# Attention and two gated layers on one core: more key tiles turned from fp32r copies, fewer rows of exponentials, query sums copied twice

## The chip, the core and the metric

One core of one Trainium2 chip runs the whole program. The metric is the device time of one execution in microseconds (us), the median of the runs shown. Engines: TensorE (PE; its weight loads are PEld), VectorE (DVE), ScalarE (ACT), GpSimd (POOL) and SyncE (SP), whose queue issues nearly all DMAs.

## What is computed

The reference, cut to what matters:

```
q, k, v: (2, 8, 1152, 64)
q_pool = q.reshape(B, H, S // 2, 2, D).mean(axis=3)
scores = (1 / sqrt(D)) * q_pool @ k.T
attn   = softmax(scores, axis=-1)
x      = (attn @ v), heads side by side      # (1152, 512)
x      = g1(x @ w_in1) @ w_out1              # 512 -> 2048 -> 512
out    = g2(x @ w_in2) @ w_out2              # the same shape, g2 = SiLU
```

There are 16 heads. Each has 576 pooled queries (four tiles of 128, and 64 that are put together with the 64 of the neighbouring head) and 1152 keys (nine tiles of 128).

## The kernel before

Every product is made in two or three fp32r matmuls of a high and a low part, so each operand is split into both parts first. The program has two halves that overlap a little: attention, to about 277 us of the span, and the two layers, which fill TensorE to the end.

Attention, per head. `inputs(h)` loads k, q and v; splits k (ACT and POOL), turns it on TensorE in three groups of three transposes and evacuates them into `kk`; adds the two query rows of a pool on POOL into one half of `qs` (line 481), copies that half into the other by a DMA (line 488), turns `qs` by four fp32 transposes (line 496) and scales and splits the outcome into `qm`. For head 0 the sum is made twice over by one DVE instruction instead of the DMA (line 483). `scores(h, t)` multiplies a query tile t with the 1152 keys in three banks (line 570), DVE evacuates them into a row tile `p` with a running minimum (line 577), and ACT takes exponentials in place (line 590). There are 8 such `p` tiles of [128, 1152] fp32, 4608 bytes a partition each, four for a head. Line 597 copies key tiles 4 and 5, and 6 to 8, of each finished `p` by DMA into `pr0` and `pr1`, which are typed fp32r: there is one buffer of each for all heads. `values(h)` goes over the nine key tiles: four transposes (one per query tile), from `p` in fp32 with `ident` (line 630) for tiles 0 to 3, from `pr` in fp32r with `ident_r` (line 634) for tiles 4 to 8; the bank is split into `thl` (ACT with DVE, or ACT with POOL), and two matmuls of 512 columns add it to the head's sum (line 647). `tails` does the same for the two joined 64-query rests, with line 676 and line 685.

Order. All instructions are first listed as operations with a due time, a cost (occupancy and latency per engine) and the buffers that they need. `plan_out` (line 265) simulates the engines with these costs and always takes what can start first, by due time among equals; the program is then written out in that order, and each engine, SP too, takes its instructions in order and waits where one is not ready. A copy of n key tiles is charged 0.2 + 0.18 n us on SP and 2.7 + 0.2 n us until it has landed; four turns from a copy are charged 0.27 us on TensorE, four from `p` 0.436 us.

The lines that the change touches:

Of the kernel before, what the change touches and what calls it, by code (L numbers as in the profile page):

```python
# [8 lines left out]
F32 = mybir.dt.float32  # L9
F32R = mybir.dt.float32r  # L10
# [8 lines left out]
def fused_kernel(  # L19
# [11 lines left out]
    nc = tc.nc  # L31
    B, H, S, D = q.shape
# [3 lines left out]
    P = 128  # L36
    KC = S // P
    NM = SQ // P
# [12 lines left out]
    THL = 4  # L51
    PF = 2
    SLACK = 0.2
    WARM = 7
    COPIED = ((4, 2), (6, 3))
    AHEAD = 3.0
    KINDS = ("psum", "pool", "psum", "pool", "psum", "pool", "psum", "pool", "pool")
    KEVAC = [[("ACT", 0.37, 0.484), ("DVE", 0.476, 0.547)]] * 3
# [8 lines left out]
    ident = const.tile([P, P], F32, name="ident")  # L67
    make_identity(nc, ident)
    ident_r = const.tile([P, P], F32R, name="ident_r")
# [72 lines left out]
    banks = [psum.tile([P, 512], F32, name=f"bank{i}") for i in range(8)]  # L142
# [103 lines left out]
    room = {}  # L246

    def op(target, ways, deps=(), bufs=(), both=False):

        if isinstance(ways, tuple):  # L250
            ways = [ways]
        o = Op(target, ways, [d for d in deps if d is not None], list(bufs), both)
        for b in o.bufs:
            b.left += 1
        ops.append(o)
        return o
# [87 lines left out]
    with ExitStack() as at, ExitStack() as keys, ExitStack() as prep:  # L344
        fixed = at.enter_context(tc.tile_pool(name="fixed", bufs=1))
        pp = at.enter_context(tc.tile_pool(name="pp", bufs=1))
# [3 lines left out]
        nat = prep.enter_context(tc.tile_pool(name="nat", bufs=1))  # L350

        def several(pool, n, shape, dt, name):
            return [pool.tile(shape, dt, name=f"{name}{i}") for i in range(n)]
# [4 lines left out]
        kraws = several(nat, 2, [P, KC, D], F32, "kraw")  # L358
        vraws = several(nat, 1, [P, KC, D], F32, "vraw")
        khls = several(nat, 2, [P, KC, 2, D], F32R, "khl")  # L360
        qss = several(nat, 2, [P, NM, 2, D], F32, "qs")
        kks = several(qk, 3, [P, KC, P], F32R, "kk")
        qms = [several(qk, 2, [P, NM * P], F32R, f"qm{i}") for i in range(2)]
        qts = [several(qk, 2, [P, 3, QT], F32R, f"qt{i}") for i in range(2)]
        ps_ = several(pp, 2 * NM, [P, S], F32, "p")
        pts = several(pp, 1, [P, S], F32, "pt")

        prs = [pp.tile([P, NM, n * P], F32R, name=f"pr{i}") for i, (_, n) in enumerate(COPIED)]
# [3 lines left out]
        y2s = several(pp, 2, [P, NM * P], F32, "y2")  # L372
        rbs = several(pp, 2, [P, NM * P], F32, "rb")
        ztail = fixed.tile([P, P], F32, name="ztail")
        tiny = fixed.tile([P, 1], F32, name="tiny")
        room.update(qraw=2, kraw=2, vraw=1, khl=2, qs=2, kk=3, qm=2, qt=2, qtraw=2, qts=1, p=2 * NM, pt=1, **{f"pr{i}": 1 for i in range(len(COPIED))}, thl=THL, pf=PF, vhl=2)
        room.update(y2=2, rb=2, z=1, b=6, y=2, w=1)

        def clear(what):
# [9 lines left out]
        khl, kk, qs, qm, qt, vhl, kraw, qraw, vraw, qtraw, o_lqt = ({} for _ in range(11))  # L389
        o_k, o_q, o_qt, o_v, o_p, o_y, o_inv, o_z = ({} for _ in range(8))  # L390
        p_of, y2_of, rb_of, pr_of, o_r = {}, {}, {}, {}, {}
# [17 lines left out]
        def inputs(h):  # L409

            b, hd = divmod(h, H)
# [15 lines left out]
            pr, odd = divmod(h, 2)  # L427
# [29 lines left out]
            for g in range(3):  # L457
                bank = Buf("b")
# [13 lines left out]
                ways = [(e, occ, lat, (lambda e=e, ev=evac: ev(e)())) for e, occ, lat in KEVAC[g]]  # L472
                o_k[h].append(op(t2 + 0.5, ways, [o], [bank, kb2]))

            qb, bank, mb = Buf("qs"), Buf("b"), Buf("qm")
            qm[h] = mb

            def split_q(e):
                t = qraws[qr.slot]
                if h:  # L480
                    e.tensor_add(qss[qb.slot][:, :, 0], t[:, :, 0], t[:, :, 1])
                else:
                    e.tensor_add(qss[qb.slot], *(t[:, :, r].unsqueeze(2).to_broadcast([P, NM, 2, D]) for r in range(2)))

            t3 = base(h - 2) - 0.1 * PERIOD
            if h:
                sq = op(t3, ("POOL", 0.7, 0.76, lambda: split_q(nc.gpsimd)), [lq], [qr, qb])
                twice = lambda: nc.sync.dma_start(out=qss[qb.slot][:, :, 1], in_=qss[qb.slot][:, :, 0])
                sq = op(t3 + 1, ("SP", 0.5, 2.6, twice), [sq], [qb])
            else:  # L490
                sq = op(t3, [("DVE", 0.6, 0.69, lambda: split_q(nc.vector)), ("POOL", 1.25, 1.31, lambda: split_q(nc.gpsimd))], [lq], [qr, qb], both=True)
            t4 = base(h - 2) + 0.3 * PERIOD

            def turn_q():
                for i in range(NM):
                    nc.tensor.transpose(banks[bank.slot][:, i * P : (i + 1) * P], qss[qb.slot][:, i].rearrange("p a d -> p (a d)"), ident)  # L496

            o = op(t4, ("PE", 0.436, 0.6, turn_q), [sq], [qb, bank])
            o1 = op(t4 + 0.5, ("ACT", 0.483, 0.62, lambda: nc.scalar.mul(qms[mb.slot][0], banks[bank.slot], SCALE)), [o], [bank, mb])

            def rest():
# [116 lines left out]
        def values(h):  # L618

            pr, odd = divmod(h, 2)  # L620
            yb = Buf("y")
            count = []
            avs = []
            for c in range(KC):
                bank, tb = Buf("b"), Buf("thl")
                tc_ = base(h) + c * STEP

                def turn(c=c, bank=bank):
                    for i in range(NM):
                        nc.tensor.transpose(banks[bank.slot][:, i * P : (i + 1) * P], ps_[p_of[h, i].slot][:, c * P : (c + 1) * P], ident)  # L630

                def turn_copy(c=c, bank=bank, x=None):
                    for i in range(NM):
                        nc.tensor.transpose(banks[bank.slot][:, i * P : (i + 1) * P].bitcast(F32R), prs[x][:, i, (c - COPIED[x][0]) * P : (c + 1 - COPIED[x][0]) * P], ident_r)  # L634

                x = [i for i, (c0, n) in enumerate(COPIED) if c0 <= c < c0 + n]
                if x:
                    do = lambda x=x[0], f=turn_copy: f(x=x)
                    o = op(tc_, ("PE", 0.27, 0.45, do), [o_r[h, x[0], i] for i in range(NM)], [bank, pr_of[h, x[0]]])
                else:  # L640
                    o = op(tc_, ("PE", 0.436, 0.6, turn), [o_p[h, i] for i in range(NM)], [bank] + [p_of[h, i] for i in range(NM)])
                parts = split(tc_ + 0.5, bank, NM, [o], tb, KINDS[c])
                for i in range(2):

                    def av(c=c, i=i, tb=tb):
                        lhsT = vhls[vhl[pr].slot][:, c, odd].rearrange("p a d -> p (a d)")
                        nc.tensor.matmul(banks[6 + yb.slot], lhsT=lhsT, rhs=thls[tb.slot][i], start=not count, stop=len(count) == 2 * KC - 1)  # L647
                        count.append(0)

                    avs.append(op(tc_ + (1.0 + i) * STEP, ("PE", 0.233, 0.41, av), [parts[i], o_v[h]], [tb, yb, vhl[pr]]))  # L650

            if not odd:
                y2_of[pr] = Buf("y2")
            yb2, fb = y2_of[pr], Buf("pf")
            src = lambda a: banks[6 + yb.slot][a * D : (a + 1) * D]
            t1 = base(h + 1) + 1.2 * STEP
            o1 = op(t1, ("ACT", 0.48, 0.6, lambda: nc.scalar.copy(pfs[fb.slot][0:D], src(1))), avs, [yb, fb])
            add = lambda: nc.vector.tensor_add(y2s[yb2.slot][odd * D : (odd + 1) * D], src(0), pfs[fb.slot][0:D])
            o_y[h] = op(t1 + 0.1, ("DVE", 0.6, 0.68, add), [o1], [yb, fb, yb2])
            if odd:  # L660
                tails(h)
# [293 lines left out]
```

## Time and profile before

| what | value |
|---|---|
| median of 3 runs | 679.89 us (678.85 to 679.95) |
| the profiled execution | 680.63 us, span 678.5 us |
| busy: PE, PEld | 670.0 us (99%), 623.5 us (92%) |
| busy: DVE, ACT, POOL | 524.0 (77%), 420.2 (62%), 438.0 us (65%) |
| DMA | 75.90 MB, mean 112 GB/s |

The span is the part of the profiled execution that its instructions cover, so 2.1 us lie around it. A busy PE is modelled: matmuls are pipelined, and the end of one is an estimate, so the distance from one start to the next says more than a duration.

### The profile page before, as it was taken

The page shows a single profiled execution, that of the slowest core. Times are in us where ns is not written, and L with a number is a line of the kernel's source. Part 1 is how long each engine was busy: PE and PEld are TensorE (multiplying, and loading weights), DVE is VectorE, ACT ScalarE, POOL GpSimd, SP SyncE. Part 2 cuts the span into 40 slices and gives each one's busy share as a digit, 9 for nine tenths or more (in the row PEclk, how much of TensorE's full clock was granted, in tenths as well). Part 3 has the DMA queues.
Part 4 walks back from the last instruction along what each step waited for, and adds up shares of the span by engine and source line. Part 5 has one row for each costly group of instructions (what it writes and reads, how often), then busy time and mean ns, then how long its engine had stood idle before and what let it go on. Part 6 is the DMA issues. An engine that isn't in the chain of part 4 may idle for free.

```text
span 678.5 us, 11815 instructions
## 1 busy us (share of the span) xinstructions
PE 670.0 (99%) x3962; PEld 623.5 (92%) x3962; DVE 524.0 (77%) x1180; ACT 420.2 (62%) x808; POOL 438.0 (65%) x414
## 2 busy tenths in 40 slices
PE   8999999999999999999999999999999999999997
PEld 6899988999999979999999999999999999999996
DVE  6879898988888898389898995996983794892223
ACT  5989998999898888455644443455554543442221
POOL 5788999999797878546646453486853553553221
PEclk8999999999999999999999999999999999999999
DMA  7866655645433356113333231231231331300012
GB/s 214 213 212 177 188 165 169 179 145 173 130 115 109 98 167 205 47 63 109 110 103 117 93 122 34 95 95 61 94 125 37 116 98 38 118 1 0 1 48 93
DMA packets 54988, 75.90 MB, mean 112 GB/s; under 512 B 14736, under 2 KB 40592, under 8 KB 54928
## 3 DMA queue, kind: packets, MB, share of 16 engines
q1 hardware_dynamic: 54640, 74.73, 35.3%
q8 instruction: 31, 0.51, 0.3%
q10 hardware_dynamic: 288, 0.43, 0.2%
q14 instruction: 29, 0.24, 0.1%
HBM read 49.81 MB, written 2.39 MB: 77 GB/s over the span
## 4 chain that ended last, share of the span: by engine, by line
PE 94%; DVE 2%; DMA 2%; ACT 1%; issue 1%; DVEq 0%; ACTq 0%
PE bank L158 30%; PE bank L203 15%; PE bank L205 15%; PE bank L570 12%; PE bank L647 10%; PE bank L630 4%; PE bank L634 3%; PE bank L685 3%; PE bank L464 1%; PE bank L676 1%; DMA pr<-p 1%; PE bank L496 1%; DMA qraw<-in_q_dram 1%; DVE p L577 0%; DVE part L217 0%
## 5 line engine op out<-in xcount | busy, mean ns | idle before, releaser
L138 POOL TENSOR_TENSOR gl<-gf,gh 128x384 fp32r<-128x384 f32 x96 | 110.0, 1147 | 107.3 <-ACT gh L187 104.0
L158 PE MATMUL bank<-xh,whi 128*128 128x384 f32 x384 | 129.7, 338 | 0.0
L158 PE MATMUL bank<-xh,wli 128*128 128x384 f32 x384 | 129.2, 337 | 0.0
L158 PE MATMUL bank<-xl,whi 128*128 128x384 f32 x384 | 129.2, 336 | 0.0
L577 DVE TENSOR_SCALAR_CACHE_REDUCE p<-bank 128x384 f32<-128x384 f32 x192 | 102.0, 551 | 20.7 <-PE bank L570 14.3
L647 PE MATMUL bank<-thl,vhl 128*128 128x512 f32 x288 | 113.4, 429 | 0.0
L138 POOL TENSOR_TENSOR thl<-pf,thl 128x512 fp32r<-128x512 f32 x80 | 103.7, 1298 | 4.0 <-PE bank L647 0.7
L181 DVE TENSOR_TENSOR gf<-bank,gf 128x384 f32<-128x384 f32 x96 | 52.9, 551 | 65.0 <-ACT gf L173 60.6
L570 PE MATMUL bank<-kk,qm 128*128 128x384 f32 x384 | 97.3, 357 | 0.3
L590 ACT ACTIVATE p<-p,low 128x1152 f32<-128x1152 f32 x64 | 81.5, 1274 | 2.7 <-DVE low L587 2.6
L187 ACT CAST gh<-gf 128x384 fp32r<-128x384 f32 x96 | 49.3, 513 | 49.6 <-DVE gf L181 47.6
L158 PEld LDWEIGHTS bank<-xl,whi 128*128 128x128 f32 x384 | 72.1, 188 | 4.2
L158 PEld LDWEIGHTS bank<-xh,whi 128*128 128x128 f32 x384 | 72.1, 188 | 4.0
L138 POOL TENSOR_TENSOR wli<-wf,whi 128x512 fp32r<-128x512 f32 x32 | 43.8, 1369 | 45.6 <-ACT whi L128 45.5
L570 PEld LDWEIGHTS bank<-kk,qm 128*128 128x128 f32 x384 | 66.4, 193 | 7.2 <-DVE thl L609 1.2
L158 PEld LDWEIGHTS bank<-xh,wli 128*128 128x128 f32 x384 | 72.1, 188 | 0.0
L138 POOL TENSOR_TENSOR wlo<-wf,who 128x512 fp32r<-128x512 f32 x32 | 44.0, 1374 | 37.3 <-ACT who L128 37.3
L173 ACT ACTIVATE gf<-bank 128x384 f32<-128x384 f32 x48 | 23.6, 491 | 70.8 <-PE bank L158 64.9
L116 DVE SCALAR_TENSOR_TENSOR wf<-wr,wf 128x512 uint32<-128x512 uint32 x56 | 65.0, 1160 | 1.0
L203 PE MATMUL bank<-gh,wlo 128*128 128x384 f32 x192 | 65.0, 338 | 0.0
L203 PE MATMUL bank<-gh,who 128*128 128x384 f32 x192 | 64.8, 337 | 0.0
L203 PE MATMUL bank<-gl,who 128*128 128x384 f32 x192 | 64.7, 337 | 0.0
(97 smaller groups left out, 1550.8 us busy)
## 6 DMA issues: line engine op xcount, KB each, us to landing
wr<-in_moe_w_in_dram SPq DMA_DIRECT2D x32, 512.0 KB, 3.7
wr<-in_moe_w_out_dram SPq DMA_DIRECT2D x32, 512.0 KB, 3.3
pr<-p SPq DMA_DIRECT2D x64, 192.0 KB, 2.3
pr<-p SPq DMA_DIRECT2D x64, 128.0 KB, 2.2
vraw<-in_v_dram SPq DMA_DIRECT2D x16, 288.0 KB, 3.3
kraw<-in_k_dram SPq DMA_DIRECT2D x15, 288.0 KB, 3.3
qraw<-in_q_dram SPq DMA_DIRECT2D x16, 256.0 KB, 3.4
rb<-row SPq DMA_DIRECT2D x16, 128.0 KB, 3.1
```

Of the source, the lines that this page charges most:

```text
L116: nc.vector.scalar_tensor_tensor(xi, st["top"], 0xC0000000, xi, ALU.bitwise_and, ALU.bitwise_or)
L138: eng.tensor_sub(out, whole, hi.bitcast(F32))
L158: nc.tensor.matmul(ps, lhsT=w[:, c, j * P : (j + 1) * P], rhs=a[:, c, ts_], start=(c == 0 and n == 0), stop=(c == ND - 1 and n == 2),)
L181: nc.vector.tensor_tensor(gf, hps.pop(i), gf, op=ALU.mult if steps[i][0] else ALU.max)
L187: nc.scalar.copy(gh, gf)
L203: nc.tensor.matmul(ps[:, :TB], lhsT=w[:, j, m * P : (m + 1) * P], rhs=a, start=start, stop=stop)
L205: nc.tensor.matmul(ps[:, cols], lhsT=a[:, m * P : (m + 1) * P], rhs=w[:, j, cols], start=start, stop=stop)
L570: nc.tensor.matmul(ps, lhsT=qq[:, c0 : c0 + P], rhs=rhs, start=n == 0, stop=n == last)
L577: nc.vector.tensor_scalar(dst, ps, -1.0, None, ALU.mult, ALU.min, accum_out=mxs[key, t][:, j : j + 1])
L590: nc.scalar.activation(pt(), pt(), AF.Exp, bias=lows[key][:, tt : tt + 1], scale=-1.0, accum_out=sums[key][:, tt : tt + 1])
L630: nc.tensor.transpose(banks[bank.slot][:, i * P : (i + 1) * P], ps_[p_of[h, i].slot][:, c * P : (c + 1) * P], ident)
L647: nc.tensor.matmul(banks[6 + yb.slot], lhsT=lhsT, rhs=thls[tb.slot][i], start=not count, stop=len(count) == 2 * KC - 1)
```

## The change

Key tiles 2 and 3 are copied too, into a `pr` buffer of their own ([128, 4, 256]), so that seven of the nine are turned from copies in fp32r. `p` has six tiles instead of eight. For all heads but the first, the query sum goes into a `qs` of half the size, and two DMAs copy it side by side into a new fp32r tile `qd`, which is turned with `ident_r`. For head 0 the sum stays fp32 and lies in the first `y2` tile until it is turned. The charge of four turns from a copy becomes 0.35 us (0.53 to the end), and that of a head's query turn too.

```
-    COPIED = ((4, 2), (6, 3))
+    STAGED, COPIED = 6, ((2, 2), (4, 2), (6, 3))
...
-        qss = several(nat, 2, [P, NM, 2, D], F32, "qs")
+        qss = several(nat, 2, [P, NM, D], F32, "qs")
+        qds = several(nat, 2, [P, NM, 2, D], F32R, "qd")
...
-        ps_ = several(pp, 2 * NM, [P, S], F32, "p")
+        ps_ = several(pp, STAGED, [P, S], F32, "p")
...
+            first_q = y2s[0].rearrange("p (t a d) -> p t a d", a=2, d=D)
...
                 if h:
-                    e.tensor_add(qss[qb.slot][:, :, 0], t[:, :, 0], t[:, :, 1])
+                    e.tensor_add(qss[qb.slot], t[:, :, 0], t[:, :, 1])
                 else:
-                    e.tensor_add(qss[qb.slot], *(...))
+                    e.tensor_add(first_q, *(...))
...
-                twice = lambda: nc.sync.dma_start(out=qss[qb.slot][:, :, 1], in_=qss[qb.slot][:, :, 0])
-                sq = op(t3 + 1, ("SP", 0.5, 2.6, twice), [sq], [qb])
+                twice = lambda: [nc.sync.dma_start(out=qds[qb2.slot][:, :, x].bitcast(F32), in_=qss[qb.slot]) for x in range(2)]
+                sq = op(t3 + 1, ("SP", 0.9, 3.0, twice), [sq], [qb, qb2])
...
                 for i in range(NM):
-                    nc.tensor.transpose(banks[bank.slot][:, i * P : (i + 1) * P], qss[qb.slot][:, i].rearrange("p a d -> p (a d)"), ident)
+                    to = banks[bank.slot][:, i * P : (i + 1) * P]
+                    if h:
+                        nc.tensor.transpose(to.bitcast(F32R), qds[qb2.slot][:, i].rearrange("p a d -> p (a d)"), ident_r)
+                    else:
+                        nc.tensor.transpose(to, first_q[:, i].rearrange("p a d -> p (a d)"), ident)
...
-            o = op(t4, ("PE", 0.436, 0.6, turn_q), [sq], [qb, bank])
+            o = op(t4, ("PE", 0.35, 0.53, turn_q) if h else ("PE", 0.436, 0.6, turn_q), [sq], [qb2 if h else qb, bank])
...
-                    o = op(tc_, ("PE", 0.27, 0.45, do), [o_r[h, x[0], i] for i in range(NM)], [bank, pr_of[h, x[0]]])
+                    o = op(tc_, ("PE", 0.35, 0.53, do), [o_r[h, x[0], i] for i in range(NM)], [bank, pr_of[h, x[0]]])
```

Nothing else changes in the text of the kernel; the order of all instructions is planned anew with these costs and buffers.

## Rows read from the trace of the kernel before

**Rows 1.** The page: busy time by engine, and the chain's shares.

```profile
PE 670.0 (99%) x3962; PEld 623.5 (92%) x3962; DVE 524.0 (77%) x1180; ACT 420.2 (62%) x808; POOL 438.0 (65%) x414
...
PE 94%; DVE 2%; DMA 2%; ACT 1%; issue 1%; DVEq 0%; ACTq 0%
```

**Rows 2.** Busy time by stretch: us, each engine's busy us, PEclk, DMA share, GB/s.

```profile
20.00:40.00 20.00, 20.00 (x136) 17.68 (x137) 16.30 (x54) 19.24 (x39) 16.44 (x18) 1.00 0.86 229
...
20.00:262.00 242.00, 240.24 (x1653) 217.92 (x1654) 209.83 (x681) 220.80 (x429) 212.78 (x215) 1.00 0.53 161
```

**Rows 3.** Timeline of TensorE, 180 to 186 us: start, us, line, operation, count.

```profile
180.21 0.60 PE L630 MATMUL bank<-ident,p 128*128 128x128 f32 x4
180.56 0.48 PE L647 MATMUL bank<-thl,vhl 128*128 128x512 f32 x1
180.88 1.03 PE L630 MATMUL bank<-ident,p 128*128 128x128 f32 x8
181.67 0.48 PE L647 MATMUL bank<-thl,vhl 128*128 128x512 f32 x1
181.99 0.33 PE L704 MATMUL bank<-jtail,ztail 128*128 128x64 f32 x2
...
183.27 0.51 PE L570 MATMUL bank<-kk,qm 128*128 128x384 f32 x2
183.62 0.40 PE L647 MATMUL bank<-thl,vhl 128*128 128x512 f32 x1
...
185.12 0.46 PE L634 MATMUL bank<-ident_r,pr 128*128 128x128 f32 x4
...
185.72 0.51 PE L570 MATMUL bank<-kk,qm 128*128 128x384 f32 x2
```

**Rows 4.** Timeline of TensorE: the first head's turns, and a pair of heads on.

```profile
20.90 2.14 PE L630 MATMUL bank<-ident,p 128*128 128x128 f32 x16
...
212.98 1.04 PE L630 MATMUL bank<-ident,p 128*128 128x128 f32 x8
```

**Rows 5.** Groups of instructions by form: count, busy us, mean ns, idle before.

```profile
L630 PE MATMUL bank<-ident,p 128*128 128x128 f32 x256 | 37.2, 273 | 0.3 <-DVE p L577 0.3
L634 PE MATMUL bank<-ident_r,pr 128*128 128x128 f32 x320 | 37.0, 239 | 0.7 <-DVE wf L120 0.6
...
L634 PEld LDWEIGHTS bank<-ident_r,pr 128*128 128x128 f32 x320 | 35.3, 140 | 5.8 <-DVE wf L120 1.0 <-DVE p L577 0.5
...
L630 PEld LDWEIGHTS bank<-ident,p 128*128 128x128 f32 x256 | 30.9, 140 | 4.3 <-DVE p L577 0.8
...
L685 PE MATMUL bank<-vhl,thl 128*128 128x256 f32 x144 | 21.9, 287 | 0.0
```

**Rows 6.** One line's instructions: duration ns min/median/max, first and last start.

```profile
L488 SPq DMA_DIRECT2D qs<-qs x15: 619/628/697, 7.5 to 199.6; - x15
L597 SPq DMA_DIRECT2D pr<-p x128: 464/521/1817, 14.1 to 262.3; - x128
```

**Rows 7.** The page: DMA queue (packets, MB, share) and issues (us to landing).

```profile
q1 hardware_dynamic: 54640, 74.73, 35.3%
...
pr<-p SPq DMA_DIRECT2D x64, 128.0 KB, 2.2
...
qs<-qs SPq DMA_DIRECT2D x15, 128.0 KB, 3.1
```

**Rows 8.** DMA issues between 20 and 40 us: KB, us to landing.

```profile
pr<-p SPq DMA_DIRECT2D x5, 128.0 KB, 3.6
```

**Rows 9.** Timelines of ACT and SP: last exponentials of two heads, and copies.

```profile
179.28 0.18 ACT L590 ACTIVATION_READ_ACCUMULATOR p<-p,low 128x1 f32 x1
...
188.11 1.31 ACT L590 ACTIVATE p<-p,low 128x1152 f32<-128x1152 f32 x1
...
179.49 1.11 SPq L597 DMA_DIRECT2D pr<-p  x2
...
20.07 1.22 SPq L597 DMA_DIRECT2D pr<-p  x2
```

More of the change, by code (lines that the diff above doesn't have):

```diff
@@ L375, in fused_kernel @@
         tiny = fixed.tile([P, 1], F32, name="tiny")
-        room.update(qraw=2, kraw=2, vraw=1, khl=2, qs=2, kk=3, qm=2, qt=2, qtraw=2, qts=1, p=2 * NM, pt=1, **{f"pr{i}": 1 for i in range(len(COPIED))}, thl=THL, pf=PF, vhl=2)
+        room.update(qraw=2, kraw=2, vraw=1, khl=2, qs=2, qd=2, kk=3, qm=2, qt=2, qtraw=2, qts=1, p=STAGED, pt=1, **{f"pr{i}": 1 for i in range(len(COPIED))}, thl=THL, pf=PF, vhl=2)
         room.update(y2=2, rb=2, z=1, b=6, y=2, w=1)
@@ L473, in inputs @@
                 o_k[h].append(op(t2 + 0.5, ways, [o], [bank, kb2]))
-            qb, bank, mb = Buf("qs"), Buf("b"), Buf("qm")
+            qb, qb2, bank, mb = Buf("qs"), Buf("qd"), Buf("b"), Buf("qm")
+            first_q = y2s[0].rearrange("p (t a d) -> p t a d", a=2, d=D)
             qm[h] = mb
@@ L480, in split_q @@
                 if h:
-                    e.tensor_add(qss[qb.slot][:, :, 0], t[:, :, 0], t[:, :, 1])
+                    e.tensor_add(qss[qb.slot], t[:, :, 0], t[:, :, 1])
                 else:
-                    e.tensor_add(qss[qb.slot], *(t[:, :, r].unsqueeze(2).to_broadcast([P, NM, 2, D]) for r in range(2)))
+                    e.tensor_add(first_q, *(t[:, :, r].unsqueeze(2).to_broadcast([P, NM, 2, D]) for r in range(2)))
             t3 = base(h - 2) - 0.1 * PERIOD
```

## The prediction

> **What bounds the kernel now.** Read the page's busy shares and chain first [rows 1]: PE is busy 99% of the span and carries 94% of the chain that ended last. A busy PE is modelled, so that alone proves little. The stretch that the change touches is attention, so the second view is busy time by stretch [rows 2]: from 20 to 262 us PE is busy 240.24 of 242 us at a granted clock of 1.00 (the 2.4 GHz level), ACT 220.80, POOL 212.78, DVE 209.83. The nearest rival has 9% to spare.
>
> The third view, TensorE's timeline, gives paces from starts [rows 3]. Four fp32 turns and one value matmul take 180.88 - 180.21 = 0.67 us; eight and one take 181.99 - 180.88 = 1.11. So four turns are 0.44, one is 0.11, and the value matmul 0.23. Two score matmuls take 183.62 - 183.27 = 0.35. Four fp32r turns and a value matmul take 185.72 - 185.12 = 0.60, so four are 0.37 and one is 0.0925.
>
> Now sum what a pair of heads must issue. By the code that is 60 score matmuls x 0.175 = 10.5, 36 value matmuls x 0.23 = 8.3, 50 fp32 turns x 0.11 = 5.5 (32 of exponentials, 8 of queries, 10 of rests), 58 fp32r turns x 0.0925 = 5.4 (40 of exponentials, 18 of keys), and 18 matmuls of the rests at no more than their busy share, 21.9 / 144 = 0.15 [rows 5], 2.7: together at most 32.4 us. The same place in the next pair starts at 212.98 [rows 4] after 180.88 [rows 3], which is 32.1 us. Work and period agree within 0.3 us: TensorE's instructions set the pace of attention, and there is hardly a wait left. A cheaper turn is therefore worth its whole pace, as long as nothing new waits.
>
> **The change part by part.**
>
> *Turns.* Key tiles 2 and 3 of 16 heads (32 groups of four) and the queries of 15 heads (15 groups) go from fp32 to fp32r: 47 groups x (0.44 - 0.37) = 3.3 us less [rows 3]. Bounds from both sides [rows 5]: the weight loads of both kinds last 140 ns, so if these set the pace the gain is 0; the modelled durations are 273 and 239 ns, and 188 x 34 ns = 6.4 us would be the most. I take 3.3, since it is read from starts on a full TensorE. The Trainium skill speaks against the gain (TensorE: Matmul & The Clock Gate, section "LDWEIGHTS"): a weight load costs its columns over 1.2, whatever else. An estimate from that is 107 ns for 128 columns in either kind, close to the 110 ns pace of the fp32 turns, and the sum would then be 0 in place of 3.3. The trace disagrees for fp32r, whose pace is 92.5 ns.
>
> *More copies.* 64 copies of two key tiles are added. On SP each costs 0.52 us of issue [rows 6], 33.4 us in all. The second copy of a query sum adds at most 0.63 x 15 = 9.4. Together 43 us, over 242 us of attention. Today's issues there are 128 x 0.52 + 15 x 0.63 = 76 us, and some 96 loads, sums and broadcasts; at between 0.3 and 0.6 each (an estimate around the two durations of [rows 6]) the queue is used 105 to 134 us, and would be used 148 to 177. It has room, so I cost it at nothing; what would be behind a late copy in SP's order is the next head's loads and query copy, needed a head later.
>
> *DMA load.* 64 x 128 KB and 15 x 128 KB are 10.4 MB more. By bytes, at 161 GB/s for a share of 0.53 [rows 2], that is 34 us of all engines, or 0.14 of the stretch. By packets (an estimate: one for each contiguous run, 64 x 128 + 15 x 512 = 15,872, at the queue's mean of 0.353 x 16 x 678.5 / 54,640 = 70 ns [rows 7]) it is 0.29. So the share becomes 0.67 to 0.82. Such a copy lands in 2.2 us at the median [rows 7] and in 3.6 where the share is 0.86 [rows 2, 8]; on a line between the two it becomes 2.8 to 3.4.
>
> *The new wait.* Turns of tiles 2 and 3 needed only the last exponentials; now they need a copy behind these. In the pair at 180 us the last exponentials of the head end at 179.46, and SP issues its last copies at 179.49 [rows 9]. Tile 2's copy, due first and so issued first, would land at 179.49 + 2.2 = 181.7, or 182.3 to 182.9 under the new load, while the third group of turns now starts at 180.88 + 0.44 = 181.32 [rows 3]. In the old order that is 0.4 to 1.6 us late. But the order is planned anew with 3.1 us from issue to landing, and next to these turns there are score and value matmuls to put in their place [rows 3]. I take 0 for the heads in the middle; the other end stands under the rivals. Behind such a turn TensorE's queue holds the next scores and values, and ACT and POOL wait for its bank.
>
> *The first head.* Its sixteen turns run as one block at 20.90 [rows 4], so tile 2's turn is at 20.90 + 0.88 = 21.8. Its last copies are issued at 20.07 [rows 9] and land in 3.6 us there [rows 8]: at best 23.7. Up to 1.9 us is open, and other heads' score matmuls fill part of it; I take 0.5 between 0 and 1.9, nearer to 0 since the stretch has no idle PE now [rows 2].
>
> *Six rows of p.* With six, a row tile can be written again only when the row six before it is let go: the third row of a head needs the first of the head before. That one is let go after the turns of its tile 1, which would end at 180.88 + 0.44 = 181.3 in the pair at 180 us [rows 3], if its copies have landed by then; the third row's exponentials start at 188.11 [rows 9]. That leaves 6.8 us for three evacuations, so I cost it at nothing. If the copies from the first row came as late as those from the last (about 182.9), 5.2 us would still be left.
>
> *The rest.* POOL's sum is the same instruction with another target. The query sum's tile is free once its copies have landed (3.1 us [rows 7]) instead of after its turn: no wait is added before a turn a head away. Head 0's sum in a `y2` tile is used long before that tile's first value. The charge of 0.35 us for turns from copies is nearer to the measured 0.37 than 0.27 was, and only changes the order; with at most 0.3 us of wait in a pair there is little for a better order to win, and I set it to 0.
>
> *Sum.* -3.3 + 0.5 = -2.8 us, all of it before the layers, which then run as now. The profiled execution of 680.63 (span 678.5 and 2.1 around it) becomes 677.8. It stands 0.7 above the median of the runs, so the median of 679.89 becomes **677.1**.
>
> **Rivals.**
>
> *Late copies: slower.* The place is the first turn from the new copy in each head. The plan counts on 3.1 us from issue to landing. Its point of decision: 3.3 us gained over 16 heads pays for 0.2 us of delay in each, so a landing over 3.3 us makes the change a loss. With the 3.6 us of the crowded stretch [rows 8] it is 0.5 us late, 15 x 0.5 = 7.5 us; 679.89 - 3.3 + 7.5 = 684.1. For it: the share rises to 0.82 by packets, and landing to 3.4 at that end. Against it: PE did not idle between 20 and 40 us, where copies already take 3.6 us [rows 2, 8], and two ready groups of turns and other matmuls stand before the late one.
>
> *Nothing measurable.* Either the weight load sets the pace of both kinds of turn (140 ns each [rows 5]), so 0 is gained (this is where the page's rule on weight loads would lead), or about two thirds of the gain goes into waits at the first and last head (up to 1.9 us each, as worked out above for the first). Time 679 to 680.5, say 679.6. For it: equal weight loads, and the block of sixteen turns. Against it: the paces in one stretch of timeline, 0.44 and 0.37.
>
> *It doesn't do what it says.* fp32r turns from copies run now and show their pace [rows 3], and the queries become the same form, so this has a chance of 0.02 and lies with nothing measurable.
>
> **How the numbers follow.** A measurement of this kernel can tell about 0.2% from no change: 1.4 us, so faster is below 678.5 and slower above 681.3. The forecast (fuller or smaller, 675.0 to 678.5) has 0.64: work and period agree so closely that the pace decides. Nothing measurable has 0.21, late copies 0.12, six rows of p that hold up a head now and then 0.03; slower is 0.15 in all. The forecast's own range is 675.0 (half of the way from 3.3 to the bound of 6.4, so 4.9 us less) to 678.5. To hold 8 in 10 it must take in nothing measurable and the beginning of late copies, so 675.0 to 681.5.
>
> **What would show it right or wrong.** Right: the period of a pair in the middle falls from 32.1 to about 31.7 us; turns of tiles 2 and 3 and of queries stand under the lines of fp32r turns at 0.37 us for four; PE stays busy over 99% from 20 to 262 us; copies land in 2.8 to 3.4 us. Wrong: idle PE or PE weight loads before turns from copies, put down to DMA or to SP's queue; a pair's period at or over 32.1; ACT waiting longer for banks of turns; DVE evacuations waiting for rows of p. The layers' part should keep its length, so a difference there would be outside this working.

## The result, and the profile after

The changed kernel takes **684.27 us** (median of 5 runs, 682.38 to 686.34) against 679.78 for the kernel before beside it: a ratio of 1.0071 [1.0056, 1.0087], so it is slower by 4.5 us. The forecast was 677.1 with a range up to 681.5, so both sign and range were wrong. The profiled execution, 686.34 us with a span of 684.4, is the longest of its five; its places are to be trusted more than its total.

First the page of the kernel after: busy time, the main DMA queue, the chain, and the landing of the two kinds of copies.

```profile
PE 671.6 (98%) x3962; PEld 621.4 (91%) x3962; DVE 521.4 (76%) x1179; ACT 420.8 (61%) x809; POOL 438.1 (64%) x414
...
q1 hardware_dynamic: 71776, 85.09, 39.4%
...
PE 88%; DVE 4%; POOL 2%; issue 2%; ACT 2%; DMA 2%; SPq 0%; DVEq 0%; POOLq 0%; ACTq 0%
...
pr<-p SPq DMA_DIRECT2D x128, 128.0 KB, 2.6
...
qd<-qs SPq DMA_DIRECT2D x30, 128.0 KB, 3.7
```

PE has as many matmuls as before [rows 1], but its share of the chain fell from 94% to 88%, and POOL is new in it with 2%. Span less PE's busy time is 684.4 - 671.6 = 12.8 us where it was 678.5 - 670.0 = 8.5. The q1 queue carries 17,136 packets more [rows 7]. A query sum's copies land 3.7 us after issue.

Now the stretches of the kernel after, in the columns of [rows 2].

```profile
20.00:40.00 20.00, 17.90 (x115) 16.02 (x114) 13.59 (x47) 15.81 (x32) 12.08 (x14) 0.91 0.77 207
...
140.00:160.00 20.00, 18.39 (x127) 15.94 (x126) 16.75 (x51) 17.14 (x35) 15.87 (x18) 1.00 0.58 188
...
20.00:262.00 242.00, 235.99 (x1615) 210.26 (x1614) 204.20 (x663) 215.45 (x419) 207.01 (x209) 0.99 0.65 198
```

PE was busy 240.24 us of the 242 before, now 235.99, with 1615 records of matmuls where there were 1653. The loss sits in places: 2.1 us of idle PE in the first row, 1.6 in the second. The DMA share over the first of these stretches is 0.77 against 0.86 before, so a higher load on the whole doesn't explain the loss. Within it the load is uneven (the profile's share can exceed 1 in a short stretch): 1.20 from 28 to 30 us and 1.14 from 30 to 31.4, just ahead of the first stop below. The kernel before has 1.16 and 1.11 from 26 to 30 us, and PE doesn't idle there.

The turns themselves did what they should. TensorE's timeline of the kernel after (start, us):

```profile
149.35 0.46 PE L640 MATMUL bank<-ident_r,pr 128*128 128x128 f32 x4
149.65 0.47 PE L653 MATMUL bank<-thl,vhl 128*128 128x512 f32 x1
149.95 0.40 PE L691 MATMUL bank<-vhl,thl 128*128 128x256 f32 x2
```

Four turns from a copy and one value matmul take 149.95 - 149.35 = 0.60 us, the figure that the prediction used for them.

Where it was lost can be followed in order of time. First SP's queue in the kernel after, 16 to 27 us:

```profile
17.14 6.24 SPq L603 DMA_DIRECT2D pr<-p  x8
...
24.11 0.41 SPq L440 DMA_DIRECT2D vraw<-in_v_dram  x1
24.61 1.31 SPq L490 DMA_DIRECT2D qd<-qs  x2
25.97 0.64 SPq L425 DMA_DIRECT2D qraw<-in_q_dram  x1
```

Then the other engines' timelines behind that load, and around a second place:

```profile
31.46 0.72 POOL L483 TENSOR_TENSOR qs<-qraw 128x256 f32<-128x256 f32 x1 [3.00 <-PE bank L576]
...
32.14 1.26 POOL L138 TENSOR_TENSOR thl<-pf,thl 128x512 fp32r<-128x512 f32 x1
...
33.44 0.59 ACT L619 COPY pf<-bank 128x512 f32<-128x512 f32 x1 [2.21 <-POOL thl L138]
...
33.46 1.22 PE L653 MATMUL bank<-thl,vhl 128*128 128x512 f32 x2 [2.10 <-POOL thl L138]
...
136.75 1.50 SPq L490 DMA_DIRECT2D qd<-qs  x2
...
142.00 0.73 POOL L483 TENSOR_TENSOR qs<-qraw 128x256 f32<-128x256 f32 x1 [1.75 <-PE bank L576]
...
144.01 0.51 PE L653 MATMUL bank<-thl,vhl 128*128 128x512 f32 x1 [1.42 <-POOL thl L138]
```

Read the first stop backwards. TensorE's value matmuls wait 2.10 us for the low parts of exponentials (`thl`, POOL L138). POOL works in order, and stood 3.00 us at the query sum ahead of them. The profile puts that wait down to PE, the last semaphore that it saw; but the load of q that SP issued at 25.97, behind a full queue, landed at 31.34, 5.4 us later, and POOL started at once. In the code the sum needs nothing from PE. How much of the 5.4 us is due to the crowded stretch isn't shown; in issue_only, a run below, the load of q issued at 28.02 landed in 3.2. At 142.00 it is the other side of the same instruction: the sum's tile was still being read by the two copies issued at 136.75, which landed at 141.35 and 141.84. A third such stop, of 1.41 us, is at 175.67; the second of that sum's copies had landed at 175.54, and TensorE waited 0.56 us behind it. The waits of the kernel after (us in total, times, longest) show POOL's first two stops and TensorE's three waits:

```profile
PEld bank L653 <- POOL thl L138: 5.2, 4, 2.4
POOL qs L483 <- PE bank L576: 4.7, 2, 3.0
PE bank L653 <- POOL thl L138: 4.1, 3, 2.1
```

The start of every 18th value matmul (a head has 18, so this is roughly where a head ends), after less before, is +3.1 us at 38 us, falls to +1.2 at 86, rises to +6.6 at 171, and is +5.9 at the last one, which ends at 281.6 us in the kernel before. The spans differ by the same 5.9, so nothing was lost in the layers.

### The profile page after: what moved, and what is told of

Same layout as the page of the kernel before. It is cut to its first block, busy times and chain, and to the rows that moved or that the text cites. A ratio compares the mean times of both kernels' runs of the same rounds, so it can differ in the third digit from the quotient of the medians.

```text
span 684.4 us, 12033 instructions
## 1 busy us (share of the span) xinstructions
PE 671.6 (98%) x3962; PEld 621.4 (91%) x3962; DVE 521.4 (76%) x1179; ACT 420.8 (61%) x809; POOL 438.1 (64%) x414
## 4 chain that ended last, share of the span: by engine, by line
PE 88%; DVE 4%; POOL 2%; issue 2%; ACT 2%; DMA 2%; SPq 0%; DVEq 0%; POOLq 0%; ACTq 0%
PE bank L158 29%; PE bank L203 15%; PE bank L205 15%; PE bank L576 10%; PE bank L653 8%; PE bank L640 4%; PE bank L691 2%; PE bank L636 2%; DVE p L583 2%; POOL thl L138 1%; PE bank L465 1%; PE bank L682 1%; DMA wr<-in_moe_w_out_dram 1%; ACT p L596 1%; DMA qraw<-in_q_dram 1%
## 5 line engine op out<-in xcount | busy, mean ns | idle before, releaser
L138 POOL TENSOR_TENSOR gl<-gf,gh 128x384 fp32r<-128x384 f32 x96 | 110.1, 1147 | 107.7 <-ACT gh L187 102.7
L138 POOL TENSOR_TENSOR thl<-pf,thl 128x512 fp32r<-128x512 f32 x80 | 103.6, 1298 | 3.2
L138 POOL TENSOR_TENSOR wli<-wf,whi 128x512 fp32r<-128x512 f32 x32 | 44.1, 1379 | 44.3 <-ACT whi L128 44.2
L138 POOL TENSOR_TENSOR wlo<-wf,who 128x512 fp32r<-128x512 f32 x32 | 44.0, 1376 | 37.0 <-ACT who L128 37.0
L620 POOL CAST thl<-pf 128x512 fp32r<-128x512 f32 x80 | 49.3, 619 | 24.4 <-ACT pf L619 15.9
```

The lines of the kernel that those rows point to most:

```text
L138: eng.tensor_sub(out, whole, hi.bitcast(F32))
L620: o1 = op(target + 0.3, ("POOL", 0.58 * f, 0.615 * f, lambda: nc.gpsimd.tensor_copy(th(), pf())), [o0], [fb, tb])
```

## The experiments

In each heading stands what was run; times are medians, ratios are to the kernel before run beside it, with the 95% interval. The expectations name their theories as these stood then.

### Which half loses: pr_only and q_only

pr_only leaves the query half as it was before (one copy, plain turns, charge 0.5 and 2.6). q_only copies five key tiles as before, with seven rows of p instead of eight, and keeps the new charge of 0.35 us for turns from copies:

```
pr_only   -  twice = lambda: [nc.sync.dma_start(out=qds[...][:, :, x]...) for x in range(2)]
          +  twice = lambda: nc.sync.dma_start(out=qss[qb.slot][:, :, 1], in_=qss[qb.slot][:, :, 0])
q_only    -  STAGED, COPIED = 6, ((2, 2), (4, 2), (6, 3))
          +  STAGED, COPIED = 7, ((4, 2), (6, 3))
```

> The exponentials' half of the change alone: seven key tiles from copies, six rows of p, the charge of 0.35 us; the query sum goes as before. Theory A (GpSimd stands at the query sums, behind the landing of the two query copies and of a late query load, and holds the low parts of thl that TensorE needs): faster than before by 32 groups x 0.07 us = 2.2 us, so about 677.5, with no wait of POOL at a query sum over 2.1 us that TensorE pays for. Theory B (64 more copies load SP's queue and the DMA engines, and this alone makes operands late): slower than before, 682 or more. Theory C (six rows of p hold up the scores): also 682 or more, with DVE evacuations waiting for rows.

> The query half of the change alone, with five key tiles from copies; p has seven rows instead of eight for want of room. Theory A: slower than before by 2 us or more (682 or more), with waits of POOL at the query sums. Theory B: 15 small copies weigh little, so 60 turns x 0.0175 = 1.0 us faster, about 678.7. Theory C: seven rows cost less than six, so near 680.

pr_only: 679.91 us, 0.999 [0.9981, 1.0]. q_only: 685.55, 1.0076 [1.0052, 1.01]. The loss comes with the query half, which has 30 of the copies; the half with 64 more copies costs nothing, but brings next to nothing of the 2.2 us that its 32 groups of turns were to bring either. q_only's timeline has the same stop:

```profile
125.34 0.72 POOL L483 TENSOR_TENSOR qs<-qraw 128x256 f32<-128x256 f32 x1 [1.91 <-DMA qd<-qs]
...
126.67 0.50 PE L653 MATMUL bank<-thl,vhl 128*128 128x512 f32 x1 [1.28 <-POOL thl L620]
```

Here the profile names the copies `qd<-qs` itself.

### The tile of the sum, and the charges: qs4, qcharge, issue_only, land_only

qs4 gives the sum four tiles in place of two. The other three change only what the plan is told of the two copies (us of SP's queue, us to land):

```
qs4          qss = several(nat, 4, ...);  room.update(... qs=4 ...)
after        sq = op(t3 + 1, ("SP", 0.9, 3.0, twice), [sq], [qb, qb2])
qcharge                      ("SP", 1.35, 4.6, twice)
issue_only                   ("SP", 1.35, 3.0, twice)
land_only                    ("SP", 0.9, 4.6, twice)
```

> The changed kernel with four query sum tiles instead of two, so that a sum need not wait for the landing of copies of the sum before. Theory A, part one (the wait is for the sum's tile): the waits at about 142 and 176 us go, 2 to 4 us less than the changed kernel, 680 to 682; the wait at 31 us, which is for the query load, stays. Theory B: no change, 684.

> The changed kernel with the plan's charge of the two query copies raised to what they took in its trace (1.35 us on SP, 4.6 us to the end, instead of 0.9 and 3.0). Theory A (the plan put the query sum too early on POOL because it thought the copies land in 3.0 us): 2 to 4 us less than the changed kernel, 680 to 682. Theory B: within 1 us of the changed kernel.

> The whole change, the query sum's two copies charged with the 1.35 us that their issue was seen to take on SP (0.9 before), the 3.0 us to land left as they are. Theory S, SP's queue: the plan sends other copies and loads too late because the issues take longer than charged; most of the 3.4 us comes back, 681 to 682 us, and q loads are no longer late. Theory T, the landing: the stops of GpSimd at query sums stay, 683.5 to 684.5 us.

> The whole change, the two copies charged with 4.6 us to land (3.0 before), the 0.9 us of issue left. Theory T: 681 to 682 us, with the waits of GpSimd at query sums under 1 us each past 100 us. Theory S: 683.5 to 684.5 us. Any new order moves the time by up to 1.8 us, so only a difference of more than that between the two runs tells the theories apart.

| kernel | us | ratio |
|---|---|---|
| qs4 | 684.54 | 1.0056 [1.0038, 1.0075] |
| qcharge | 681.07 | 1.0 [0.9987, 1.0013] |
| issue_only | **677.79** | **0.9967 [0.9955, 0.998]** |
| land_only | 682.31 | 1.0041 [1.0028, 1.0055] |

With four tiles the stops at 142 and 176 us are gone, as theory A expected, but the time is the same. The first stop, at the load of q, is there as in the kernel after and is longer in this order (3.40 us for 3.00), as qs4's timeline shows; so the sum's tile is not all of the loss:

```profile
32.74 0.72 POOL L483 TENSOR_TENSOR qs<-qraw 128x256 f32<-128x256 f32 x1 [3.40 <-DMA qraw<-in_q_dram]
...
34.74 1.22 PE L653 MATMUL bank<-thl,vhl 128*128 128x512 f32 x2 [2.50 <-POOL thl L138]
```

Charging both copies as measured brings back 3.2 us (684.27 - 681.07), and the charge of the issue alone more than that: issue_only is faster than the kernel before by 2.5 us and than the change by 6.5 (684.27 - 677.79, of different batches; by the kernel before beside each it is 7.0), and it is the same instructions in another order. That is under the ranges of both theories. land_only, 2.0 us better than the change, lies between the ranges of its two theories; it has no stop at a sum past 100 us, but one of 2.04 us at 29.99. What one such issue takes on SP, by line, in the kernel after and in issue_only (duration ns min/median/max):

```profile
L490 SPq DMA_DIRECT2D qd<-qs x30: 608/631/1840, 7.2 to 204.7; - x30
```

```profile
L490 SPq DMA_DIRECT2D qd<-qs x30: 619/631/726, 7.3 to 196.9; - x30
```

Two are 1.26 us, and 1.3 from first start to last end (24.61 above); the change charged 0.9. The page, the stretch, the turns by form and two timelines of issue_only:

```profile
PE 667.2 (99%) x3962; PEld 619.8 (92%) x3962; DVE 522.3 (77%) x1177; ACT 421.1 (62%) x811; POOL 437.8 (65%) x414
...
PE 93%; DVE 3%; ACT 2%; DMA 1%; issue 1%; POOL 0%; DVEq 0%; ACTq 0%; POOLq 0%
...
qd<-qs SPq DMA_DIRECT2D x30, 128.0 KB, 3.0
```

```profile
20.00:262.00 242.00, 239.96 (x1668) 216.21 (x1667) 209.95 (x681) 223.31 (x434) 216.27 (x219) 1.00 0.69 206
```

```profile
L640 PE MATMUL bank<-ident_r,pr 128*128 128x128 f32 x448 | 51.3, 240 | 0.3 <-DVE thl L615 0.2
...
L500 PE MATMUL bank<-ident_r,qd 128*128 128x128 f32 x60 | 6.9, 238 | 0.0
```

```profile
26.65 1.33 SPq L490 DMA_DIRECT2D qd<-qs  x2
28.02 0.64 SPq L425 DMA_DIRECT2D qraw<-in_q_dram  x1
...
36.61 0.75 POOL L483 TENSOR_TENSOR qs<-qraw 128x256 f32<-128x256 f32 x1
```

PE is busy 239.96 us of 242 as before, now with 1668 records of matmuls. Span less busy PE is 675.7 - 667.2 = 8.5, the same as before, and busy PE fell from 670.0 to 667.2: 2.8 us less work and no more idle time. All 448 + 60 turns from copies are there. In this order the query sum stands 36.61 - 28.02 = 8.6 us behind the issue of its load, where the kernel after had 31.46 - 25.97 = 5.5, and POOL does not stop: no bracket follows the row. It stops at one sum only, at 151.68 us for 1.22, put down to the copies `qd<-qs`, and no matmul waits behind that.

One thing speaks against a simple reading. If the right charge of the issue were all, qcharge should be as fast, and it is 3.3 us slower. Its order has other waits, the largest 1.57 us on PE at 133.5. A plan of this kind turns any number into another order, and orders differ by themselves; the next runs say by how much.

### What an order is worth: charge_only, spare_copy, q_old_order, pool_twice

charge_only is the kernel before with nothing but the change's new charge for turns from copies. spare_copy is the kernel before, in its old order, with a second copy of each query sum that nobody reads. q_old_order is the whole change in the order planned as if the query half were the old one. pool_twice lets POOL write the sum twice over, so that one copy of longer rows does.

```
charge_only  -  op(tc_, ("PE", 0.27, 0.45, do), ...)
             +  op(tc_, ("PE", 0.35, 0.53, do), ...)
spare_copy   +  twice = lambda: [nc.sync.dma_start(out=o, in_=qss[...][:, :, 0]) for o in (spare, qss[...][:, :, 1])]
q_old_order  +  sq = op(t3 + 1, ("SP", 0.5, 2.6, twice), [sq], [qb])      # qb2 = qb in the plan
pool_twice   +  e.tensor_add(qss[qb.slot], *(t[:, :, r].unsqueeze(2).to_broadcast([P, NM, 2, D]) ...))
             +  sq = op(t3 + 1, ("SP", 0.6, 3.0, twice), [sq], [qb, qb2])      # one copy
```

> The kernel before with nothing changed but the plan's charge for turns from copies (0.35 us instead of 0.27, 0.53 to the end). It shows what planning the order anew is worth by itself. My theory has it within 1 us of before; if an order planned anew can by itself cost some us, then part of the loss needs no other cause.

> The kernel before with one more copy of each query sum into a tile that nobody reads, in the unchanged order (15 more DMAs of 128 KB in pieces of 256 bytes, and the sum's tile is free only after both). Theory A1: within 1 us of before. Theory A2: 2 us slower or more.

> The whole change, but in the order that was planned for the exponentials' half alone: the plan sees the query sum, its copy and its turn with the charges and the one tile of before, while the kernel issues both copies and turns from the fp32r tile. Theory A1 (the loss lies in the order, planned with a copy charge that was too short, so that GpSimd and TensorE come to the query sum and turn too early): as the exponentials' half alone or up to 1 us better, 679 to 680. Theory A2 (the second copy itself does it, by SP's queue and the DMA engines): 682 or more, with POOL waiting at query sums.

> The changed kernel with the query sum written twice over by GpSimd (1.25 us in place of 0.7 by the plan) and one DMA of 2 KB a partition into the fp32r tile instead of two in pieces of 256 bytes, charged 0.6 and 3.0 us. Theory A: the copy lands in about 2.5 us instead of 3.7, inside its charge, and the waits at the query sums behind landings go: 679 to 681. If GpSimd's 8 us more of work bind instead: 683 or more.

| kernel | us | ratio |
|---|---|---|
| charge_only | 682.3 | 1.0026 [1.0015, 1.0037] |
| spare_copy | 681.8 | 1.0021 [1.0009, 1.0032] |
| q_old_order | 686.42 | 1.0085 [1.0071, 1.01] |
| pool_twice | 681.3 | 1.0014 [1.0003, 1.0024] |

charge_only adds no instruction and costs 682.3 - 680.55 = 1.75 us, more than the 1 us expected: that is the price of a new order alone. It was set to 0 in the prediction.

spare_copy tells what SP's queue does with issues that the plan doesn't know. It is 1.25 us slower, between the two theories, and the distance is reached by 36 us and constant from there on. The copies of exponentials that SP issues at 20.07 us in the kernel before [rows 9] are issued 1.2 us later here, which is two of the spare issues (at 12.61 and 17.29). Its SP and TensorE timelines:

```profile
21.27 2.61 SPq L598 DMA_DIRECT2D pr<-p  x2
...
25.74 0.62 PE L635 MATMUL bank<-ident_r,pr 128*128 128x128 f32 x5 [1.03 <-DMA pr<-p]
...
28.04 0.28 PE L635 MATMUL bank<-ident_r,pr 128*128 128x128 f32 x1 [0.66 <-DMA pr<-p]
```

So an uncharged issue of 0.63 us a head is paid where SP has work without a gap, and free later. q_old_order goes further that way: its pair of copies is charged at 0.5, and it is the slowest of all. Its order is that of pr_only, operation by operation, so the 6.5 us between the two (686.42 - 679.91, of different batches; 6.4 by the kernel before beside each) are the query half's own and not a new order's. By 75 us its values are 7.2 us behind those of the kernel before. Its waits have the late copies of exponentials in them, which the kernel after had not:

```profile
PE bank L641 <- DMA pr<-p: 3.0, 3, 1.5
```

Here the theory fell that the change would do well if only the order were left alone. pool_twice has no stop left behind a copy, only 1.9 us behind loads of q; its copy landed in 3.1 us at the median, not 2.5, and its time is 0.3 us above the range expected.

### Plans with longer landings: true_before, true_pr, true_after, true_twice

All four are planned with loads 1 us longer and copies of exponentials at 3.6 + 0.2n (was 2.7 + 0.2n); the query sum's copies at 0.65 and 3.6 (true_before, true_pr), 1.35 and 4.6 (true_after), 0.65 and 4.0 (true_twice). true_before is the kernel before, true_pr has seven tiles copied, true_after is the whole change, true_twice is pool_twice.

```
-  ("SP", 0.2 + 0.18 * n, 2.7 + 0.2 * n, copy)
+  ("SP", 0.2 + 0.18 * n, 3.6 + 0.2 * n, copy)
```

> The kernel before, planned with the same longer landings: the control. It has hardly a wait for a landing to lose, so both theories have it within 1.5 us of before; if it gains as much as the other two, their gain is the order's and not the change's.

> The exponentials' half alone, planned with the same longer landings (the one query copy 0.65 and 3.6). Theory A: 677 to 679, below the 679.9 of the same half with the old charges. Theory B: no better than 679.9.

> The whole change, planned with the times to landing of its own trace: loads 1 us longer (k, q and v 4.8 to 4.9, the rest of q 4.3), copies of exponentials 3.6 + 0.2 n instead of 2.7 + 0.2 n, the two query copies 1.35 and 4.6. Theory A (an order planned with landings that are too short puts GpSimd and TensorE behind DMAs that have not landed): the waits for landings go and the change keeps its cheaper turns, 677 to 679, faster than both kernels. Theory B (the added DMAs themselves are too much): 681 or more, as with the query charge alone.

> The form in which GpSimd writes the query sum twice over and one DMA copies it (681.3 with the old charges), planned with the longer landings, the copy 0.65 and 4.0. Theory A: 677 to 679. Theory B: 681 or more.

| kernel | us | ratio |
|---|---|---|
| true_before | 681.83 | 1.0023 [1.0013, 1.0033] |
| true_pr | 681.51 | 1.0012 [1.0003, 1.0022] |
| true_after | 680.53 | 0.9993 [0.9985, 1.0002] |
| true_twice | 682.19 | 1.0024 [1.0015, 1.0032] |

No theory's gain came: true_after lies between its two ranges, true_pr and true_twice are in those of theory B. The longer landings made the unchanged work slower by 1.3 us, true_pr by 1.6 against pr_only and true_twice by 0.9 against pool_twice; only the whole change gained (684.27 to 680.53). Planned alike, the whole change is worth 681.83 - 680.53 = 1.3 us, and its seven tiles 0.3; both are within what a new order alone was seen to cost.

### Is the crowded start to blame: late_after, late_pr, late_qcharge, later_qcharge

Tiles 2 and 3 are copied only from head 3 on (later_qcharge: head 5); until then they are turned from `p`.

```
+  if i == 0 and h < 3: continue
...
-  x = [i for i, (c0, n) in enumerate(COPIED) if c0 <= c < c0 + n]
+  x = [i for i, (c0, n) in enumerate(COPIED) if c0 <= c < c0 + n and (i or h >= 3)]
```

> The whole change, but heads 0 to 2 (numbers as in the code) turn key tiles 2 and 3 straight from p as before; from head 3 on all seven tiles are copied. Theory E, the crowded start is paid for: up to 75 us SP issues 3 or so fewer copies of 128 KB; 2 to 3 us come back, 681 to 682.5 us, and the waits of TensorE ahead of 75 us are near those of before. Theory L, the loss is made later, where GpSimd stops at query sums (142 and 176 us): the time stays within 1 us of 684.3, with the same waits of GpSimd past 100 us.

> The query half left as before (one copy, two plain turns); seven tiles copied from head 3 on, five until then. Theory E: 678 to 679.5 us, 1 to 2 under the 679.9 of seven tiles from the first head. Theory L: 680 us, no change, as the waits at query sums were not there to begin with.

> As the run before it, and the query sum's two copies charged with 1.35 us of issue and 4.6 us to land. Theory E: the waits at query sums go with the charge and the start is eased as well, 678 to 680 us, under the kernel before. Theory L: the charge alone did it, 681 us as without the easing.

> The charged query half, and tiles 2 and 3 copied only from head 5 on. Theory E: past 75 us nothing more is eased, and two more heads go without the quicker turns of two groups each: 0.3 us over the version from head 3 on, 678.5 to 680.5 us. Theory L: 681 us.

late_after 683.48, 1.0039 [1.0027, 1.0051]; late_pr 680.2, 0.9996 [0.9988, 1.0005]; late_qcharge 680.88, 1.0007 [0.9998, 1.0015]; later_qcharge 680.83, 1.0002 [0.9993, 1.0011]. Against the same kernels with all heads alike that is 0.8 us less, 0.3 more, 0.2 less and 0.2 less. Theory E fell: fewer copies at the start bring little. The stop near 31 us is gone in late_after, but the stops at the later query sums stay where the charge is the old one (144 and 176 us, and a new one at 44), as its timeline shows:

```profile
143.99 0.73 POOL L483 TENSOR_TENSOR qs<-qraw 128x256 f32<-128x256 f32 x1 [1.65 <-DVE bank L108]
...
145.33 0.51 PE L655 MATMUL bank<-thl,vhl 128*128 128x512 f32 x1 [0.71 <-POOL thl L622]
```

### All runs with two copies of the query sum

Eleven kernels issue the pair and turn from it. The charge of its 1.3 us of issue divides them:

```
charged 0.5 or 0.9:  after 684.27, land_only 682.31, late_after 683.48, qs4 684.54, q_only 685.55, q_old_order 686.42
charged 1.35:        issue_only 677.79, qcharge 681.07, late_qcharge 680.88, later_qcharge 680.83, true_after 680.53
```

The groups don't overlap, and their medians (684.4 and 680.83) are 3.6 us apart. This division was made after the fact. Within each group the times still spread, by 4.1 and 3.3 us. spare_copy, which issues a pair charged 0.5 and turns nothing from the second copy, has 681.8. And four of the five with 1.35 are charged a longer landing too, so the groups alone don't tell the two charges apart.

The plan can be asked as well, for `plan_out` gives every operation a time. The column "planned" is worked out from the listing of each kernel and is not measured: where the last value matmul of a head ends. Beside it stands the same place in the profiled execution, whose first issue on SP starts 0.7 us later than the plan's (us; in brackets the pair's charges):

| kernel | planned | profiled | behind its plan |
|---|---|---|---|
| after (0.9, 3.0) | 280.61 | 287.51 | 6.90 |
| land_only (0.9, 4.6) | 279.53 | 280.24 | 0.71 |
| qcharge (1.35, 4.6) | 280.46 | 283.33 | 2.87 |
| issue_only (1.35, 3.0) | 279.27 | 278.81 | -0.45 |
| pr_only | 280.47 | 279.11 | -1.36 |
| q_old_order | 280.47 | 286.87 | 6.40 |
| charge_only | 283.13 | 283.27 | 0.14 |

charge_only runs as planned: what it costs is in its plan. The kernel after doesn't run as planned, and issue_only does. Their plans differ by 1.3 us at this place, and the rest of the 8.7 us between the two profiled executions is lateness against the plan. But land_only, with the short charge of the issue, is hardly late either, so which of the two charges took the lateness away is not shown.

## Why the prediction was wrong

**Turns: right.** The pace of four copied turns holds in the kernel after (0.60 us with a value matmul). In the order that adds no idle time, issue_only, the saving is 2.8 us of PE's busy time and 2.5 us of time, where 3.3 and, less the first head, 2.8 had been worked out. Some of these 2.5 us may not be the turns': TensorE's clock was granted at 0.91 over the first 20 us of the profiled kernel before and at 1.00 in issue_only, and issue_only is already 0.7 us ahead when the first head ends, at 35 us. The rule of the Trainium skill that was weighed there (TensorE: Matmul & The Clock Gate, section "LDWEIGHTS"), that a weight load costs its columns, and so the same in both kinds of turn here, would have given no gain; the pace in the kernel after does not bear it out.

**The rest: the step that failed.** It said of the query sum that its tile is free once its copies have landed and that "no wait is added before a turn a head away". The turn does not wait. What waits is the next sum on POOL, for that tile and for its own load; and behind a sum POOL's queue holds the low parts of exponentials that TensorE's next value matmuls need. The text asked only who reads the new copy, not what stands behind the instruction that refills its source. The kernel after has POOL stopped at three sums for 3.00, 1.75 and 1.41 us, and PE's waits for `thl` behind them add up to 4.1 us. q_only puts 5.1 us on this half (685.55 - 680.41), with the new charge and seven rows in it; q_old_order against pr_only, in one order, puts 6.5.

**More copies: counted, but not set against the charge.** "At most 0.63" for the second copy was right (0.631), and so was the sum: SP had room on the whole. But the change charges a pair at 0.9, and 2 x 0.63 stood in the prediction's own rows; the two were not compared. In an order planned ahead a queue's lateness does not need a full queue; it needs a stretch without gaps, as SP's between 12 and 36 us, and a waiter without slack. spare_copy shows it by itself (+1.25 us), and issue_only shows what the right charge brings. That the whole 6.5 us between after and issue_only is this charge is not shown, since qcharge, charged no less, keeps 3.3 of them. Nor is the pair the only wrong charge: a load of q is charged 1.1 us on SP and took 0.57 at the median, so the queue also gains time on its plan. The load of the first stop was planned to be issued at 24.2 us and to land at 28.0; it was issued at 26.0 and landed at 31.3. So 1.8 us of its 3.4 are the issue's (0.7 of that because SP's first issue starts 0.7 us into the span), and 1.6 the landing's.

**Replanning set to 0: wrong.** charge_only costs 1.75 us and true_before 1.3 without any new work. A step of up to 1.8 us belonged in the working of a change whose gain was put at 2.8.

**DMA load: right in size, wrong as the worry.** The share became 0.65 where 0.67 to 0.82 was expected, and the copies of exponentials land in 2.6 us (2.8 to 3.4 expected). The point of 3.3 us for the rival of late copies was not reached, at the median, by the copies that the rival spoke of.

**The new wait, the first head, six rows of p.** No wait of TensorE for copies of tile 2 is among the larger ones in the kernel after, and pr_only, with six rows and seven tiles, costs nothing. These zeros hold: of the signs that were named, PE's busy share fell (235.99 of 242 us), but only 0.5 us of idle time in all stand ahead of turns from copies. But pr_only was expected faster than 679.91: its 2.2 us came out at 0.5, and at 0.3 in true_pr against true_before. Where they went isn't settled. In pr_only's profiled execution, one of its fastest (678.79), PE has more matmul records in the stretch (1664 in 240.01 us busy), and the last value matmul ends 2.5 us earlier than in the kernel before; the span is only 1.5 us shorter.

**The rival that had the time.** "Late copies: slower" gave 684.1, 0.2 us off, for a mechanism in another place: at turns of tile 2, not at the sums. Its number was right by chance. What came true was a cousin of it: loads and copies that are issued and land later than planned decide, through POOL.

**Open.** By the plans, 1.3 us of issue_only's lead over the kernel after are its luck among orders. Whether the charge of the issue would take the lateness away in other orders too could be told only by many orders with each charge. Why landings of one and the same transfer differ so much (5.4 us for the load of the first stop, 3.2 at the median of that load) was not tested.

## What to carry to other kernels

Where the order of instructions is planned from charges, compare every charge, for issue and for landing, with the duration in the trace, queue by queue; a pair of DMA issues charged a third too low was in the rows here. Then compare the planned time of an operation with the measured one: it parts an order that is longer by plan from one that runs late. For a new copy ask what refills its source, on which engine, and what is queued behind that instruction. And take two or three orders of the same work before judging a change worth 0.4%: the same instructions ran in 677.8 and in 684.3 us.

## What the hardware did that was not expected

A copy of 128 KB between two SBUF tiles landed later, at the median, with 256-byte pieces than with rows of 1 KB: 3.7 against 2.6 us in the kernel after, 3.1 against 2.2 in the kernel before [rows 7]; in issue_only the two are nearly alike (3.0 and 2.9). The moment of issue and the load beside it were not held constant, so that the pieces are the cause is not shown. The Trainium skill says that transfers between SBUF tiles don't suffer the penalty of small descriptors (DMA: Bandwidth & Descriptors, section "Why small descriptors are slow (HBM only)"); no run here decides it.

The first stop cost more than its idle time. In the stretch around its end the granted clock was 0.54 on the mean, near the 1.2 GHz level; the kernel after, in the columns of [rows 2]:

```profile
33.00:36.00 3.00, 2.54 (x10) 2.24 (x11) 0.34 (x2) 1.95 (x5) 2.87 (x5) 0.54 0.83 271
```

PE had been idle for 2.1 us up to 33.46. Idle PE was followed by slow PE here, and in this execution the wait at POOL cost more than the 2.1 us that stand beside it. In qs4 it is the same behind the stop of 2.50 us (0.50 from 34.74 to 37.74). Behind the shorter stop at 144.01 the kernel after keeps 1.00 (144 to 147 us), and issue_only, without a stop, has 1.00 in the stretch above.
